# Attention and a two-part mixer: the channel mixer's pace in batches 2 and 3, and the row order of four heads' loads

## The chip, the cores and the metric

The kernel runs on one core of one Trainium2 chip. The metric is the device time of one launch in microseconds. Before the change it is 367.9 us, the median of 13 runs (366.7 to 375.08). The core's engines are TensorE (PE in the profile, with its weight loads as PEld), VectorE (DVE), ScalarE (ACT), GpSimd (POOL) and SyncE (SP); each takes its instructions in order and waits for the others by semaphores.

## The reference

Eight batches of eight heads, 576 tokens, head width 64. Causal attention with a decay bias is followed by a mixer over the sequence (low rank, 32) and a mixer over the channels:

```python
scores = scale * np.matmul(q, k.transpose(0, 1, 3, 2))
cum = np.cumsum(np.maximum(s, 0.0), axis=-1)
bias = -(cum[:, :, :, None] - cum[:, :, None, :])
scores = np.where(causal, -1e9, scores + np.minimum(bias, 0.0))
attn = softmax(scores)                    # with the row maximum and 1e-9
x = (attn @ v) heads side by side         # (8, 576, 512)
h = x.transpose(0, 2, 1) @ U @ V
u = x + h.transpose(0, 2, 1)
out = u + np.maximum(u @ w_ch1, 0.0) @ w_ch2      # 512 -> 2048 -> 512
```

Inputs and output are float32; the kernel works in bf16 and collects in float32.

## The kernel before, in words

**Attention** goes by pairs of heads, `n` = 0 to 31, four pairs a batch. `transposes(n)` turns q and k of a pair on TensorE (L314, 16 matmuls of 72 columns) into two PSUM banks; four copies on VectorE or ScalarE bring them to the pair's slot (L334 or L337). Which of the two lines runs depends on how q and k were loaded: in 72-token runs (L111: a partition holds tokens p, p + 72, and so on, in pieces of 64 numbers) the copy is straight (L334); with eight neighbouring tokens to a partition (L116: one piece of 512 numbers) the copy must put the tokens in order by a stride (L337). `in_runs` (L105) chooses, and is true for batches 3 to 7. For n = 4, 8, 9 and each batch's pair n % 4 == 2 above 8, ScalarE makes the copies of the first head. `scores(n)` is four steps of score matmuls (L401), each with an exponential on ScalarE (L416, L427, L433) and, for three of them, a causal mask on VectorE (L346). `values(n)` is two steps (one a head) of 15 matmuls (L461), each emptied by a reciprocal and a product on VectorE (L470, L471).

**The sequence mixer** `seqmix(b)` works on one batch: a product with U (L490), a small turn (L503), then the wide product with V (L535) into one score tile and two PSUM banks, and its last 64 tokens (L560). VectorE casts between them (uxT, L499; ux, L505) and adds x at the end (L515), which makes uT.

**The channel mixer** `chanmix(g)` works on groups of 512 tokens, nine in all, of which group b is complete when `seqmix(b)` is. It has 30 steps for groups 1 to 7. Sixteen are the *first product*: four matmuls of 512 columns (L647), then a ReLU on ScalarE (L807). Fourteen are the *second product*, done as seven products of half-size blocks (L692), eight matmuls of 256 columns to a step, with sums of blocks ahead of them (L674) and adds of results and of u behind them (L706), all on VectorE. Group 1's first eight steps also carry eight sums of weights on VectorE (L256). Each group's results go out from SP's queue (L716).

**Order.** PE's, VectorE's and the other engines' queues are in order. Attention's order is written out: up to pair 9 as words in `weave`, from `n = 8` on by the loop at L1008, which for each n takes transposes of n + 1, scores of n and values of n - 1. The channel mixer fills in between: after each attention step `step_fill` (L852) adds `pace[1]` to a counter and runs one channel mixer step whenever it reaches 16. So a pace of 11 gives 11 channel mixer steps to 16 attention steps. A batch's sequence mixer stands beside the next batch's second pair (`hp == 1`): its first two steps between attention steps, its other four with one channel mixer step after each (`fill_with(1)`). After it the next group is put on the list. What is left of the channel mixer when attention is done runs alone at the end.

**Buffers.** PSUM has four banks of one kind (`pwork`), shared by transposes, the scores' last piece, values, both channel products and the sequence mixer, and two score tiles of two banks each (`pscore`). q and k have two buffers each, filled a batch ahead from GpSimd's queue (L111, L116) with v behind them (L185); the loads for batch 2 are in two halves of four heads (`load(2)`, L965).

Of the kernel before, what the change touches and what calls it, by code (L numbers as in the profile page):

```python
# [39 lines left out]
def kernel(  # L40
# [40 lines left out]
    def pwork():  # L81
        return ps_w.tile([128, 512], FP32, tag="w", name="pwork")
# [19 lines left out]
        q_t[b] = loads.tile([TP, H, TT * D], BF16, tag="q_sd", name="q_sd")  # L102
        k_t[b] = loads.tile([TP, H, TT * D], BF16, tag="k_sd", name="k_sd")

    def in_runs(b):  # L105
        return b > 2

    def load_qk(b, h, n):
        for dst, src in ((q_t[b], q), (k_t[b], k)):
            if in_runs(b):  # L110
                nc.gpsimd.dma_start(  # L111
                    out=dst[:, ds(h, n), :].rearrange("p h (t d) -> p (h t) d", t=TT),
                    in_=src[b, ds(h, n)].rearrange("h (t p) d -> p (h t) d", p=TP),
                )
            else:
                nc.gpsimd.dma_start(  # L116
                    out=dst[:, ds(h, n), :],
                    in_=src[b, ds(h, n)].rearrange("h (p t) d -> p h (t d)", p=TP),
                )
# [6 lines left out]

    alloc_qk(0)
    load_qk(0, 0, 2)
    identity = consts.tile([128, 128], BF16)
    make_identity(nc, identity)  # L130
    load_qk(0, 2, 2)
    load_qk(0, 4, 2)
    load_qk(0, 6, 2)

# [44 lines left out]
    def load_v(b, parts=range(5)):  # L179
        vt = v_slot(b)  # L180
        if b < 3:
            init_v(nc.gpsimd, vt)
        for t in parts:
            rows_t = 128 if t < 4 else 64
            nc.gpsimd.dma_start(  # L185
                out=vt[:rows_t, t, :, 0:D],
                in_=v[b, :, ds(t * 128, rows_t), :].rearrange("h p d -> p h d"),
            )
# [14 lines left out]
    def slot_of(n):  # L203
        return slots[n % NSLOT if n < 2 * PB else (n + 1) % 3]
# [8 lines left out]
    def spin(n, dst):  # L213
        for _ in range(n):
            nc.tensor.matmul(  # L215
                dst, lhsT=busy[:, 0:128], rhs=busy[:, 0 : dst.shape[1]], start=True, stop=True
            )
# [70 lines left out]
    def copies(n, hh, par):  # L288
        b = n // PB
        on_act = hh == (n == 4) and ((n in (0, 1, 4, 8, 9) or n > 8 and n % PB == 2) or n == 2 and par == 0)  # L290
        return nc.scalar.copy if on_act else nc.vector.tensor_copy

    def transposes(n):
        b, hp = divmod(n, PB)
        slot = slot_of(n)
        if b > 0:
            for r, n_r, c in ((0, 3, 1), (3, 1, 0)):
                nc.sync.dma_start(
                    out=slot[ds(D + r, n_r), :, ds(c * S, S)],
                    in_=rows_hbm[ds(r, n_r), ds(2 * n, 2)],  # L300
                )
        tps = {}

        def turn(hh, c):
            if c == 0:
                tile = pwork()
                if (n, hh) == (3, 0):
                    spin(2, tile)
                tps[hh] = tile.bitcast(BF16)[:, : 2 * 4 * TP].rearrange(
                    "p (c t m) -> p c t m", c=2, t=4  # L310
                )
            src = (q_t[b], k_t[b])[c]
            for t2 in range(4):
                nc.tensor.transpose(  # L314
                    tps[hh][:, c, t2, :],
                    src[:, 2 * hp + hh, ds(t2 * 128, 128)],
                    identity[:TP, :TP],
                )

        if b == 0:  # L320
            for hh in range(2):
                turn(hh, 0)
            yield
        for hh in range(2):
            if b > 0:
                turn(hh, 0)
            turn(hh, 1)
            tp = tps[hh]
            dst = slot[0:D, hh, 0 : 2 * S]
            for par in range(2):  # L330
                src = tp[par * D : par * D + D]
                if in_runs(b):
                    by_run = dst.rearrange("p (c t two m) -> p c t two m", c=2, t=4, two=2)
                    copies(n, hh, par)(by_run[:, :, :, par, :], src)  # L334
                else:
                    in_turn = dst.rearrange("p (c m t two) -> p c m t two", c=2, t=4, two=2)
                    copies(n, hh, par)(  # L337
                        in_turn[:, :, :, :, par], src.rearrange("p c t m -> p c m t")
                    )
            yield  # L340
# [56 lines left out]
    def scores(n, pT, spins=()):  # L397
        slot = slot_of(n)

        def mm(dst, hh, j, lo, hi):  # L400
            nc.tensor.matmul(  # L401
                dst,
                lhsT=slot[0:KA, hh, ds(S + j * 128, 128)],
                rhs=slot[0:KA, hh, lo:hi],
                start=True,
                stop=True,
            )

        tail = None
        for hh in range(2) if n > 0 else ():  # L410
            near = pscore()
            for j in range(4):
                mm(near[:, ds(j * 128, 128)], hh, j, j * 128, j * 128 + 128)
            mm(near[:, 512:960], hh, 0, 128, S)
            mm(near[:, 960:1024], hh, 3, 512, S)
            nc.scalar.activation(pT[:, hh, 0:1024], near, EXP, scale=scale)  # L416
            if n >= PB:
                mask(pT[:, hh, 0:512].rearrange("p (a b) -> p a b", a=4), 4, 128)
            if spins:
                tail = tail or pwork()  # L420
                spin(spins[hh], tail)
            yield
        mid, tail = pscore(), tail or pwork()
        for hh in range(2):
            mm(mid[:, ds(hh * 512, 320)], hh, 1, 256, S)
            mm(mid[:, ds(hh * 512 + 320, 192)], hh, 2, 384, S)
        nc.scalar.activation(  # L427
            pT[:, :, 1024:1536], mid.rearrange("p (a b) -> p a b", a=2), EXP, scale=scale
        )
        yield  # L430
        for hh in range(2):
            mm(tail[:, ds(hh * 64, 64)], hh, 4, 512, S)
        nc.scalar.activation(  # L433
            pT[:, :, 1536:1600],
            tail[:, 0:128].rearrange("p (a b) -> p a b", a=2),
            EXP,
            scale=scale,
        )
        if n >= PB:
            mask(pT[:, :, 1536:1600], 2, 64)  # L440
        yield
# [408 lines left out]
    pace = [0, 16]  # L850

    def step_fill():  # L852
        pace[0] += pace[1]
        if pace[0] < 16:
            return
        pace[0] -= 16
        while fill:
            if next(fill[0], fill) is not fill:
                return
            fill.pop(0)  # L860

    def run(gen):
        for _ in gen:
            step_fill()
# [5 lines left out]
    def fill_with(n):  # L870
        per, pace[1] = pace[1], 16
        for _ in range(n):
            step_fill()
        pace[1] = per


    def pT_of(n):
        if n < PB + 3:
            return pTs[n % 2] if n % PB < 2 else pT_early[n % PB - 2]
        return pTs[(n + 1) % 2]  # L880

    def step(*gens):
        for gen in gens:
            next(gen, None)
# [80 lines left out]
    def load(b):  # L965
        alloc_qk(b)
        for h in range(0, H, 4 if b == 2 else H):
            load_qk(b, h, 4 if b == 2 else H)
# [35 lines left out]
    weave("V4 V4 S7 V5 S7 V5 S7 V6 S7 V6 T8 T8 V7 S8 V7 S8 T9 S8 T9")  # L1004
    weave("S8 S9 M1 S9 M1 S9 M1 M1 S9 M1 F M1")
    fill.append(chanmix(1))
    pace[1] = 11
    for n in range(2 * PB, NP + 2):  # L1008
        b, hp = divmod(n, PB)
        if hp == 0 and b < B - 1:  # L1010
            load(b + 1)
        mixing = seqmix(b - 1) if hp == 1 and b > FT else iter(())
        if b == B:
            fill_with(3)
            for _ in range(3):
                step(mixing)
                fill_with(2)
        if n > 2 * PB and n + 1 < NP:
            for at, _ in enumerate(transposes(n + 1)):
                step_fill()  # L1020
                if at == 0:
                    step(mixing)
        if 2 * PB + 1 < n < NP:
            for at, _ in enumerate(scores(n, pT_of(n))):
                step_fill()
                if at == 1:
                    step(mixing)
        for _ in mixing:
            fill_with(1)
        if hp == 1 and b > FT:  # L1030
            fill.append(chanmix(b - 1))
            pace[1] = 12
        if 2 * PB < n <= NP:
            run(values(n - 1, pT_of(n - 1)))
        if hp == 0 and 2 <= b < B - 1:
            load_v(b + 1)
# [35 lines left out]
```

The softmax here doesn't subtract the row's maximum and nothing guards it: scores larger than these inputs give would overflow.

## Time and profile before

| what | us |
|---|---|
| median of 13 runs | 367.9 |
| the profiled execution's own time | 368.34 |
| its span (first to last instruction) | 366.6 |
| PE busy | 356.3 |
| VectorE busy | 262.2 |
| ScalarE busy | 204.5 |
| GpSimd busy | 83.4 |
| L647, 560 matmuls of the first product | 136.3 |
| L692, L674, L706: the second product on PE, its sums and its adds on VectorE | see the groups by line |

A busy time is the sum of an engine's instructions, overlaps counted once. A group's row has the line, engine and operation, the tiles as out<-in with their shapes, the count, then busy us and mean ns of one, and behind the last bar the idle time ahead of these instructions with what ended it. A timeline's row has start and length in us; "x4" means four instructions of the kind in a row, and the bracket is the idle time before the first and what released it. Matmuls overlap in the pipeline and their ends are modelled, so PE's pace is read from starts.

### The profile page before, as it was taken

To read this page: it belongs to the slowest core of one execution; us is meant where nothing else is said; L and a number is where in the kernel's file an instruction comes from. 1 tells how busy PE (TensorE), PEld (TensorE's weight loads), DVE (VectorE), ACT (ScalarE), POOL (GpSimd) and SP (SyncE) were. 2 spreads that over 40 slices of the span, in tenths; PEclk is the share of its full clock that TensorE was granted. 3 is DMA by queue.
4 is the path that set the end of the run, shared out by engine and by line. 5 is a ranking of instruction groups with operands and counts; after the bars stand their busy time and mean duration, and the time that the engine had idled before them with its cause. 6 is when DMAs were issued, how large, how long until landed. Compare 5 with 4: busy or idle time off the path is not lost.

```text
span 366.6 us, 9426 instructions
## 1 busy us (share of the span) xinstructions
PE 356.3 (97%) x3959; PEld 248.6 (68%) x3959; DVE 262.2 (72%) x575; ACT 204.5 (56%) x309; POOL 83.4 (23%) x108
## 2 busy tenths in 40 slices
PE   8899999999999999999999999999999999999995
PEld 4675566665588667876679667876697568477484
DVE  8865776779798758995699559974897178076075
ACT  3874985756663578347843786357734630631720
POOL 8988435314030403140214022000000000000000
PEclk9999999999999999999999999999999999999999
DMA  7999999999949899989994999361014202403202
GB/s 109 168 205 201 165 192 104 147 129 142 98 44 91 145 142 63 99 90 115 140 100 65 142 132 84 58 156 22 18 48 118 64 18 84 91 5 109 61 29 88
DMA packets 147650, 37.40 MB, mean 102 GB/s; under 512 B 130648, under 2 KB 145976, under 8 KB 147608
## 3 DMA queue, kind: packets, MB, share of 16 engines
q0 software_dynamic: 104640, 18.49, 78.6%
q1 hardware_dynamic: 42680, 18.11, 27.3%
q8 instruction: 31, 0.51, 0.6%
q10 hardware_dynamic: 288, 0.20, 0.2%
q14 instruction: 11, 0.09, 0.1%
HBM read 37.25 MB, written 9.70 MB: 128 GB/s over the span
## 4 chain that ended last, share of the span: by engine, by line
PE 77%; DVE 12%; ACT 5%; issue 2%; DMA 2%; SPq 0%; DVEq 0%; ACTq 0%
PE pwork L647 29%; PE pwork L692 21%; PE pscore L401 9%; PE pwork L461 7%; PE pwork L314 3%; PE pwork L657 3%; DVE slot L337 2%; ACT hT L807 2%; DVE uT L515 2%; DVE o_sb L706 2%; ACT pT L416 2%; DVE slot L674 2%; DMA slot<-hT 2%; PE pscore L215 1%; PE pscore L647 1%
## 5 line engine op out<-in xcount | busy, mean ns | idle before, releaser
L647 PE MATMUL pwork<-uT,w_sb 128*128 128x512 bf16 x560 | 136.3, 379 | 1.5 <-DVE x_sb L471 0.8
L807 ACT ACTIVATE hT<-pwork 128x512 bf16<-128x512 f32 x140 | 84.3, 606 | 62.3 <-PE pwork L647 62.2
L416 ACT ACTIVATE pT<-pscore 128x1024 bf16<-128x1024 f32 x56 | 57.1, 1030 | 55.8 <-PE pscore L401 54.8
L647 PEld LDWEIGHTS <-w_sb 128*128 128x128 bf16 x576 | 50.7, 97 | 51.0 <-issue 1.2
L401 PE MATMUL pscore<-slot 68*128 68x320 bf16 (+1 forms) x500 | 56.1, 246 | 1.1 <-DMA slot<-hT 0.9
L401 PEld LDWEIGHTS <-slot 68*128 68x128 bf16 x564 | 41.3, 97 | 17.8 <-issue 1.3
L692 PEld LDWEIGHTS <-hT 128*128 128x128 bf16 x496 | 46.1, 98 | 7.5 <-issue 0.7
L185 POOL DMA_DIRECT2D v_slot<-in_v_dram x36 | 30.3, 857 | 85.2 <-PE pwork L461 74.6
L692 PE MATMUL pwork<-w_sb,hT 128*128 128x256 bf16 x384 | 47.5, 273 | 0.0
L346 DVE TENSOR_TENSOR pT<-pT,keep 128x512 bf16<-128x512 bf16 (+1 forms) x81 | 28.6, 353 | 20.7 <-ACT pT L416 14.9
L461 PEld LDWEIGHTS <-pT 128*128 128x128 bf16 x870 | 32.4, 97 | 5.3 <-issue 0.6
L461 PE MATMUL pwork<-v_slot,pT 128*128 128x65 bf16 x870 | 35.5, 194 | 0.2 <-DVE uT L515 0.2
L334 DVE COPY slot<-pwork 64x576 bf16<-64x576 bf16 x70 | 31.6, 452 | 4.5 <-PE pwork L314 3.9
L692 PE MATMUL pwork<-w_sum,slot 128*128 128x256 bf16 x256 | 31.5, 273 | 0.8 <-DVE o_sb L706 0.7
L471 DVE TENSOR_TENSOR x_sb<-pwork,rec 128x320 bf16<-128x320 f32 x64 | 31.1, 489 | 1.3
L337 DVE COPY slot<-pwork 64x576 bf16<-64x576 bf16 x35 | 28.0, 801 | 5.5 <-PE pwork L314 3.5
L427 ACT ACTIVATE pT<-pscore 128x1024 bf16<-128x1024 f32 x29 | 30.2, 1042 | 2.6 <-PE pscore L401 2.4
L674 DVE TENSOR_TENSOR slot<-hT 128x1024 bf16<-128x1024 bf16 x16 | 11.0, 688 | 24.5 <-ACT hT L807 24.3
L470 DVE RECIPROCAL rec<-pwork 128x5 f32<-128x5 f32 x64 | 12.0, 190 | 22.2 <-PE pwork L461 21.9
L692 PEld LDWEIGHTS <-slot 128*128 128x128 bf16 x256 | 24.0, 98 | 4.6 <-issue 1.6
L706 DVE TENSOR_TENSOR o_sb<-o_sb,pwork 128x512 f32<-128x512 f32 (+2 forms) x34 | 21.9, 650 | 1.0 <-PE pwork L692 0.3
L111 POOL DMA_DIRECT2D q_sd<-in_q_dram x5 | 11.2, 2239 | 43.0 <-PE pwork L314 43.0
(128 smaller groups left out, 417.5 us busy)
## 6 DMA issues: line engine op xcount, KB each, us to landing
out_dram<-o_sb SPq DMA_DIRECT2D x35, 256.0 KB
w_sb<-in_moe_w_ch_dram POOLq DMA_DIRECT2D x4, 1024.0 KB, 12.4
v_slot<-in_v_dram POOLq DMA_DIRECT2D x28, 128.0 KB, 6.8
q_sd<-in_q_dram POOLq DMA_DIRECT2D x5, 576.0 KB, 14.2
k_sd<-in_k_dram POOLq DMA_DIRECT2D x5, 576.0 KB, 17.6
q_sd<-in_q_dram POOLq DMA_DIRECT2D x4, 288.0 KB, 11.9
k_sd<-in_k_dram POOLq DMA_DIRECT2D x4, 288.0 KB, 11.6
q_sd<-in_q_dram POOLq DMA_DIRECT2D x4, 144.0 KB, 4.5
```

The source lines that it names most:

```text
L185: nc.gpsimd.dma_start(out=vt[:rows_t, t, :, 0:D], in_=v[b, :, ds(t * 128, rows_t), :].rearrange("h p d -> p h d"),)
L334: copies(n, hh, par)(by_run[:, :, :, par, :], src)
L337: copies(n, hh, par)(in_turn[:, :, :, :, par], src.rearrange("p c t m -> p c m t"))
L401: nc.tensor.matmul(dst, lhsT=slot[0:KA, hh, ds(S + j * 128, 128)], rhs=slot[0:KA, hh, lo:hi], start=True, stop=True,)
L416: nc.scalar.activation(pT[:, hh, 0:1024], near, EXP, scale=scale)
L427: nc.scalar.activation(pT[:, :, 1024:1536], mid.rearrange("p (a b) -> p a b", a=2), EXP, scale=scale)
L461: nc.tensor.matmul(po[:, i, :], lhsT=pT[:, hh, ds(place(j, i), 128)], rhs=vt[:, j, h, :], start=(j == 0), stop=(j == i), skip_group_check= ...
L471: nc.vector.tensor_tensor(x_sb[:, hp, :, ds(hh * D, D)], po[:, :, 0:D], rec.to_broadcast([128, 5, D]), op=ALU.mult,)
L647: nc.tensor.matmul(f1, lhsT=w1_sb[:, kt, ds(nf * 128, 128)], rhs=u[:, kt, :], start=(kt == 0), stop=(kt == 3),)
L692: nc.tensor.matmul(acc[:, i, :], lhsT=a[:, kt, ds(i * 128, 128)], rhs=b[:, kt, :], start=(i == 0 and kt == 0), stop=(kt == HF - 1), skip_g ...
L706: nc.vector.tensor_tensor(dst, a, b, op=ALU.add)
L807: nc.scalar.activation(hT[:, nf, :], f1, RELU)
```

## The change

Three things are changed. The pace of group 1's channel mixer during batch 2 goes from 11 to 6. The pace from batch 3's sequence mixer slot on (group 2) goes from 12 to 10, and stays 12 from batch 4's on. Heads 4 to 7 of batch 2 (pairs 10 and 11) are loaded in 72-token runs, as batches 3 to 7 are, so that their copies are the straight ones; heads 0 to 3 stay as they were.

```diff
-    def in_runs(b):
-        return b > 2
+    def in_runs(b, h):
+        return b > 2 or b == 2 and h >= 4
...
         for dst, src in ((q_t[b], q), (k_t[b], k)):
-            if in_runs(b):
+            if in_runs(b, h):
                 nc.gpsimd.dma_start(
...
                 src = tp[par * D : par * D + D]
-                if in_runs(b):
+                if in_runs(b, 2 * hp):
                     by_run = dst.rearrange("p (c t two m) -> p c t two m", c=2, t=4, two=2)
...
     fill.append(chanmix(1))
-    pace[1] = 11
+    pace[1] = 6
     for n in range(2 * PB, NP + 2):
...
         if hp == 1 and b > FT:
             fill.append(chanmix(b - 1))
-            pace[1] = 12
+            pace[1] = 10 if b < 4 else 12
         if 2 * PB < n <= NP:
```

## Prediction

> **What bounds the kernel now.** I read the page's first part, then its groups by line, then a table of busy time by stage, and last the timeline of the stages that were not full.
>
> ```profile
> PE 356.3 (97%) x3959; PEld 248.6 (68%) x3959; DVE 262.2 (72%) x575; ACT 204.5 (56%) x309; POOL 83.4 (23%) x108
> L334 DVE COPY slot<-pwork 64x576 bf16<-64x576 bf16 x70 | 31.6, 452 | 4.5 <-PE pwork L314 3.9
> L337 DVE COPY slot<-pwork 64x576 bf16<-64x576 bf16 x35 | 28.0, 801 | 5.5 <-PE pwork L314 3.5
> ```
>
> TensorE (PE) is issued nearly without a break, and the change neither adds nor removes a matmul. So the time can only move by PE's waits. The same copy of transposed q and k costs VectorE (DVE) 801 ns by stride (L337) and 452 ns in runs (L334).
>
> The stage table (stretch, its length, then busy time of PE, PEld, DVE, ACT, POOL) shows where PE waits:
>
> ```profile
> 78.50:102.30 23.80, 22.76 (x263) 13.90 (x261) 20.73 (x44) 16.27 (x26) 4.45 (x2) 1.00 1.96 117
> 102.30:118.00 15.70, 15.42 (x211) 13.39 (x210) 13.81 (x33) 7.85 (x12) 4.23 (x5) 1.00 0.86 68
> 118.00:141.00 23.00, 23.00 (x258) 14.93 (x256) 16.64 (x41) 15.50 (x25) 4.47 (x2) 1.00 1.51 134
> 182.00:195.00 13.00, 12.70 (x171) 10.80 (x170) 11.82 (x28) 5.20 (x8) 2.82 (x4) 1.00 1.24 87
> 220.00:234.00 14.00, 13.59 (x174) 11.11 (x171) 13.02 (x31) 5.84 (x10) 2.27 (x3) 1.00 0.98 78
> 256.00:270.00 14.00, 13.51 (x168) 10.07 (x165) 12.18 (x28) 7.95 (x13) 0.00 (x0) 1.00 0.06 13
> ```
>
> The first row is batch 2 beside group 1's first product, with DVE at 87%. The others that are not full hold a sequence mixer each, with DVE at 87 to 93%; between them (118 to 141) PE is full. The ends of matmuls are modelled and hide some 0.16 us of each wait, so I measure a wait from start to start: four 128x512 matmuls take 0.86 us, eight 128x256 take 0.88, a 15-matmul half of the values 0.46, four transposes 0.13, scores of a pair 1.38.
>
> ```profile
> 90.39 0.30 PE L314 MATMUL pwork<-identity,q_sd 72*128 72x72 bf16 x4
> 90.52 0.29 PE L314 MATMUL pwork<-identity,k_sd 72*128 72x72 bf16 x4
> 91.41 1.04 PE L647 MATMUL pwork<-uT,w_sb 128*128 128x512 bf16 x4 [0.60 <-DVE x_sb L471]
> ```
>
> ```profile
> 186.93 0.68 DVE L706 TENSOR_TENSOR o_sb<-U,u_sd 128x512 f32<-128x512 f32 x1
> 187.53 0.69 DVE L674 TENSOR_TENSOR v_slot<-hT,slot 128x1024 bf16<-128x1024 bf16 x1
> 188.13 0.22 DVE L346 TENSOR_TENSOR pT<-pT,keep 128x128 bf16<-128x128 bf16 x1
> 188.26 1.28 DVE L515 TENSOR_TENSOR uT<-pscore,xT 128x512 bf16<-128x512 f32 x2
> 189.46 0.75 DVE L515 TENSOR_TENSOR uT<-pwork,xT 128x256 bf16<-128x256 f32 x2
> 190.12 0.68 DVE L706 TENSOR_TENSOR o_sb<-o_sb,pwork 128x512 f32<-128x512 f32 x1
> ```
>
> At 90.52 the transposes would be through at 90.65; the next matmul starts at 91.41, so 0.76 us lost, because DVE had only just emptied the PSUM bank. At 188 the sequence mixer's uT adds stand in one queue with the second product's adds; the matmul that needs that bank starts at 190.85, 0.47 late.
>
> Such waits in all: batch 2 0.28 (80.3), 0.33 (83.3), 0.76 (90.6), 0.33 (99.8) = **1.7 us**; around sequence mixers 0.25 (112.8), 0.35 (116.9), 0.47 (190.4), 0.58 (230.2), 0.66 (261.8), 0.25 (302.8) = 2.56, of which 0.1 is a change of tile rows that stays: **2.45 us**. This 4.15 us is all that there is to win after 78 us; before that nothing is changed on PE.
>
> **What the Trainium skill says.** "TensorE: Matmul & The Clock Gate", section Back-to-back issue gap, gives N/2.4 + 2.5 ns between matmuls, 216 ns for 512 columns; the trace has 0.86/4 = 0.215 and agrees. (The shorter 131 ns that the section gives for streams with weight loads is not seen here.) "VectorE: DVE Perf Modes", What auto-detection actually checks, lets an all-16-bit op run at two elements a cycle only with step 1; the 801 against 452 ns above agree. "DMA: Bandwidth & Descriptors", Why small descriptors are slow, puts some 27% on a 256-byte piece: the direction agrees, the size I take from the trace below. "Perfetto Trace Analysis" calls matmul busy time a bad metric for closeness to the limit; hence starts, not busy shares, above.
>
> **The change part by part.** *Pace 6 for 11 in batch 2.* In the order of the built program, at the wide step of batch 2's sequence mixer (L535), group 1 has had 16 + 7 steps before the change and 13 after it: ten fewer. They move to the end of the program, where the last groups run alone at 0.86 and 0.88 us a step without gaps (the chain shows 64 matmuls in 13.81 and 112 in 12.23 us there): cost **0**, as PE does the same work.
>
> In batch 2 a pair now carries 3 steps of the first product and not 5.5. PE per pair: values 0.92, transposes 0.51, scores 1.38, 3 x 0.86 = 5.4 us. DVE per pair, in start-to-start distances read off its timeline (a row's mean is longer, since its ops overlap by 0.07 to 0.1): masks 0.34 + 0.34 + 0.14, values' reciprocals and products 1.04, copies 4 x 0.46, weight sums (L256) 3 x 0.60 = 5.5 us. So DVE keeps step within 2%. Before it had 0.82 + 1.04 + 4 x 0.80 + 5.5 x 0.60 = 8.4 against 7.6 of PE, and the 3 us by which it was behind at 92 us is what PE paid for. New there: ScalarE (ACT) gets a string of exponentials. From the end of the first score block to the bank that the first product wants after the values, ACT has 0.91 (exp) + 0.50 (ReLU) + 0.91 + 0.91 + 0.24 + 0.50 = 3.97 us after a start 0.2 later, PE 3.83: 0.35 late, once per pair, three times: 1.0 us. Batch 2: 1.7 becomes 1.0, **-0.7 us**.
>
> *Runs for pairs 10 and 11.* Eight copies; six on DVE fall from 0.80 to 0.46 = -2.0 us of DVE, two on ACT. Without it DVE would need 6.9 us in pair 11 against 5.4, so it is what makes the line above hold; no gain of its own beyond that. Cost: two loads (q and k, heads 4 to 7, 288 KB each) become 4608 rows of 256 bytes. Gpsimd issues them in about half of L111's 2.24 us each for eight heads, against 0.72: 2 x 0.4 = 0.8 us on a queue that waits anyway. On the DMA engines: from 55.4 (last piece of v for batch 2) to 83.7 us (v of batch 3 landed) q, k and v of batch 3, some 13,800 such rows, landed, 2.0 us a thousand, so 9.4 us; the long rows gave up 576 KB, which at the weight loads' 1024 KB in 12.4 us is 7.0. Net **+2.4**, bounded by 0 below and 9.4 above. What covers it: behind them are v of batch 2 (lands at 64.7, wanted at 79.9), and q and k of batch 3 (k issued at 59.97, lands 17.6 later at 77.6; wanted, in the new order, 7.7 us of PE after 78.5, so 86.2). The smaller slack is 8.6 us; the loads themselves land by 58.9, wanted at 78.5. Cost 0, at the upper end 0.8 us.
>
> *Every later sequence mixer* stands in the first product: in the built order the seven uT adds on DVE are now consecutive in all mixers from batch 2 to 7, and in most of them the cast ux stands ahead of any sum; before, 2 to 4 adds or sums of 0.6 us stood in between. Behind L535 PE now has three to four first-product steps, 2.6 to 3.5 us, which want ACT; the adds take 2.9 us on DVE. So 2.45 us of waits go. What is late next: the product steps all stand beside attention pairs, at pace 10 and 12. Per group DVE has 17 adds and sums x 0.605 = 10.3 plus 2.33 to 2.8 pairs x 3.7 = 18.9 to 20.7 us, PE 18.8 to 20.1: level, as before (19.4 against 19.0). I walked both orders with these distances, each engine taking its list in turn, and added how late each bank comes: before 6.8 us outside batch 2, of which the trace shows 2.85 with its small waits (0.42); after 4.4 us, spread as 0.4 to 0.6 over eight places, at the same ratio 1.85. That is -1.0; the count of waits removed says -2.45 at most. I take **-1.3**.
>
> *Pace 10 in batch 3* only keeps this offset. Queue order on SP: out stores move with the products, nobody waits for them.
>
> Sum: -0.7 - 1.3 = -2.0 us. The profiled run took 368.34 (span 366.6 and 1.7 around it), 0.44 above the median of 367.9; so 366.3 on its scale, **365.9** as a median.
>
> **Rivals.**
> (a) The waits change place only: ACT's string in batch 2 and the product steps beside scores cost what the mixers gave back. For: DVE's level load per group above; against: the uT run without sums. At no more than -0.7: 367.2 to 367.9, taken as 367.5.
> (b) Slower: DVE becomes the bound of the product phases, which now have none of their steps in a mixer's shadow. If its ops cost their full rows (0.69 an add, 4.2 a pair), DVE has 11.7 + 2.5 x 4.2 = 22.2 us against 19.3 of PE per group; once more than some 2 us behind (the time in which PE refills the four banks), PE pays about 1 us in each of groups 1 to 4: +4.0 - 0.7 (batch 2) - 1.0 (mixers) = +2.3, 370.2. Against it: back-to-back distances in DVE's timeline are 0.60, and before had the same load.
> (c) Larger gain: nearly all 4.15 go, and ACT's string hides in buffers: -3.8, 364.1.
> (d) The loads in runs come late: decides above 8.6 us, at most 0.8; an addition to any case, not a case.
>
> **How the numbers follow.** Forecast 0.41, (c) 0.15, (a) 0.28, (b) 0.16. About 0.5% (1.84 us) is what a measurement of this kernel can tell from no change. Forecast and (c) are faster by over that, just so for the forecast; hence 0.56, 0.28, 0.16. The range takes in (a), most of (c) and the near part of (b): 363.8 to 369.2. The forecast's own range is 364.8 to 366.6.
>
> **What would show it.** Right: PE full in the stretches of the mixers; seven uT adds in a row with no L706 or L674 among them; no L337 copy on DVE after batch 2's first two pairs and DVE below 95% there; T12's transposes not waiting for a DMA. Wrong: L692 waiting for DVE beside scores and values (b), L647 waiting for ACT L807 after values at many pairs (a), or PE waiting for k_sd at about 86 us (d).

## The result and the profile after

The changed kernel takes 371.35 us as a median (11 runs, 368.98 to 377.81) against 367.34 for the kernel before (48 runs). The ratio is 1.0091, interval 1.0071 to 1.0111: slower by some 3.3 us, where 2.0 us less was forecast. Medians and ratios differ a little because executions in which the chip was disturbed count in the medians, not in the ratios.

The profiled execution took 370.23 us (span 368.5), 1.1 below its median, while the one of before lay 1.0 above its own. So the two traces show only 1.9 us of the loss, and I use them for places and mechanisms; sizes come from the timed runs.

The page's busy row and the two copy rows of the kernel after:

```profile
PE 357.4 (97%) x3959; PEld 247.9 (67%) x3959; DVE 261.5 (71%) x575; ACT 203.8 (55%) x309; POOL 84.7 (23%) x108
L334 DVE COPY slot<-pwork 64x576 bf16<-64x576 bf16 x76 | 34.3, 451 | 2.5 <-PE pwork L314 1.6
L337 DVE COPY slot<-pwork 64x576 bf16<-64x576 bf16 x29 | 23.3, 802 | 5.1 <-PE pwork L314 3.3
```

The instructions are the same in number. Six copies on VectorE moved from L337 to L334 and cost what they cost before. So nothing was added to the work; PE waits more.

The table by stage of the kernel after (stretch, length, busy of PE, PEld, DVE, ACT, POOL, then clock, DMA share, GB/s). The stretches are those of before by work: batch 2, its sequence mixer, the stretch behind it, then the sequence mixers of batches 4, 5 and 6:

```profile
78.00:98.00 20.00, 19.77 (x273) 13.35 (x272) 17.98 (x48) 16.13 (x25) 5.21 (x3) 1.00 2.15 128
98.00:112.00 14.00, 11.91 (x150) 8.03 (x148) 10.93 (x27) 7.63 (x13) 3.47 (x5) 1.00 1.63 79
112.00:135.00 23.00, 23.00 (x328) 18.87 (x325) 19.90 (x48) 13.07 (x19) 7.81 (x6) 1.00 1.57 148
170.00:184.00 14.00, 12.82 (x133) 6.95 (x132) 7.13 (x20) 9.20 (x16) 2.71 (x4) 1.00 1.25 111
206.00:220.00 14.00, 13.99 (x173) 9.15 (x170) 9.70 (x25) 8.15 (x13) 4.22 (x5) 1.00 1.22 151
244.00:258.00 14.00, 14.00 (x177) 10.00 (x174) 11.39 (x29) 7.32 (x11) 0.00 (x0) 1.00 0.50 107
```

The last two rows are what was forecast: mixers in which PE is busy throughout and VectorE at 69 and 81%. The second and the fourth are the surprise. PE is idle for 2.1 and 1.2 us there, while VectorE is at 78% and 51%. No engine is the bound in these stretches.

The list of waits of the kernel after, from 78 us on, names what is late (who <- for what: us in all, times, longest). The list of before has no row in which anything waits for xT:

```profile
DVE uT L515 <- DMA xT<-x_sb: 3.7, 2, 2.1
...
PEld L461 <- DVE uT L515: 3.1, 2, 1.6
...
PE pwork L461 <- DVE uT L515: 2.3, 2, 1.2
```

xT is x turned by a DMA: behind the values of each pair SP issues a DMA transpose (L478, in the last lines of `values`) into the pair's fourth of xT, and the uT adds of the sequence mixer add it. At two mixers the last pair's fourth was not there when its three adds came up. VectorE's timeline shows both places:

```profile
103.83 1.28 DVE L515 TENSOR_TENSOR uT<-pscore,xT 128x768 bf16<-128x768 f32 x2
105.03 0.74 DVE L515 TENSOR_TENSOR uT<-pwork,xT 128x384 bf16<-128x384 f32 x2
107.35 1.09 DVE L515 TENSOR_TENSOR uT<-pwork,xT 128x384 bf16<-128x384 f32 x3 [1.58 <-DMA xT<-x_sb]
...
176.54 1.28 DVE L515 TENSOR_TENSOR uT<-pscore,xT 128x512 bf16<-128x512 f32 x2
177.74 0.74 DVE L515 TENSOR_TENSOR uT<-pwork,xT 128x256 bf16<-128x256 f32 x2
180.61 1.09 DVE L515 TENSOR_TENSOR uT<-pwork,xT 128x256 bf16<-128x256 f32 x3 [2.13 <-DMA xT<-x_sb]
```

The seven adds do stand in a row, as the built order said. Their first four run; the last three wait. The bank that they should empty is wanted next by the values. PE's timeline of the kernel after, at both places:

```profile
105.96 1.04 PE L692 MATMUL pwork<-w_sb,hT 128*128 128x256 bf16 x8
108.16 1.09 PE L461 MATMUL pwork<-v_slot,pT 128*128 128x65 bf16 x30 [1.17 <-DVE uT L515]
...
110.10 0.29 PE L314 MATMUL pwork<-identity,k_sd 72*128 72x72 bf16 x4
110.77 1.05 PE L692 MATMUL pwork<-w_sb,hT 128*128 128x256 bf16 x8 [0.38 <-DVE x_sb L471]
...
179.27 1.03 PE L647 MATMUL pwork<-uT,w_sb 128*128 128x512 bf16 x4
181.42 1.09 PE L461 MATMUL pwork<-v_slot,pT 128*128 128x65 bf16 x30 [1.13 <-DVE uT L515]
```

From start to start, 105.96 to 108.16 is 2.20 against 0.88, so 1.3 us lost, and 179.27 to 181.42 is 2.15 against 0.86, again 1.3. At 110.10 the transposes take 0.67 instead of 0.13: VectorE, set back by its wait, is late with the next bank as well.

Why is x's transpose late? The chain that ended last, in the window of each mixer, gives the way from issue to landing (start, length, what):

```profile
98.19 8.69 DMA xT<-x_sb
...
171.54 8.98 DMA xT<-x_sb
```

Around the second of them, SP's queue of the kernel after reads:

```profile
168.44 3.00 SPq L814 DMA_TRANSPOSE u_sd<-uT  x1
171.54 1.58 SPq L478 DMA_TRANSPOSE xT<-x_sb  x1
```

and in the kernel before, at the same mixer, nothing stands ahead of the last x:

```profile
181.99 1.24 SPq L478 DMA_TRANSPOSE xT<-x_sb  x1
```

VectorE's last three adds start there without a wait:

```profile
190.72 1.08 DVE L515 TENSOR_TENSOR uT<-pwork,xT 128x256 bf16<-128x256 f32 x3
```

In the kernel before, x's last values were ready at 181.96 and the transpose went out at 181.99. In the kernel after they were ready at 169.44 and it went out at 171.54, 2.1 us later, because SP was inside the transpose of u (L814). The channel mixer issues that in its fourth step (`nf == 3`), so it goes wherever the pace puts that step; here it fell just ahead of the last x.

The wait on SP is only half of it. The trace also records when a DMA has completed. In the kernel before, this x landed at 189.08, 7.1 us after its issue; in the kernel after at 180.52, 9.0 us after it. The DMA packets show what lay between: u's 2048 pieces of 256 bytes run from 169.7 to 174.3 us, and x's 640 only from 175.6 to 178.2. From x ready to x landed that makes 7.1 us before and 11.1 us after.

At batch 2's mixer nothing stood ahead on SP (98.17 ready, 98.19 issued). There the DMA engines were full. GpSimd's queue of the kernel after shows when the loads were issued:

```profile
83.59 2.22 POOL L111 DMA_DIRECT2D k_sd<-in_k_dram  x1
97.25 4.22 POOL L185 DMA_DIRECT2D v_slot<-in_v_dram  x5 [11.43 <-PE pwork L461]
```

The view of the DMAs gives 19.7 us from issue to landing for this k load (batch 4's), so until 103.3; v, which waits for the same last values as x, goes out beside it and takes 9.3 us at the median. v goes out beside x (108.19) in the kernel before too:

```profile
106.40 4.23 POOL L185 DMA_DIRECT2D v_slot<-in_v_dram  x5 [18.18 <-PE pwork L461]
```

What differs is the k load. In the kernel before the same view, from 94 to 107 us in 40 slices, has the DMA engines' busy tenths as

```profile
DMA  9999999999999999999510399400000000000002
```

so they were idle from 102.5 us until v went out, and x's turn came at 108.19; it landed 5.3 us later. From the issue of that k load to x's last transpose there were 22.2 us before (86.00 to 108.19) and are 14.6 now. The Trainium skill, "Perfetto Trace Analysis", Per-instruction lifecycle, warns that for a DMA the whole data movement lies outside the instruction's row. This case agrees: SP's row at 98.19 is 1.22 us, the data came 8.69 us after it began. Nor is it a matter of the transpose's rate: "DMA: Bandwidth & Descriptors", Latency and other measured facts, has 261 GB/s for a DMA transpose, by which the 160 KB of one pair (128 partitions x 640 bf16) would move in an estimated 0.6 us. No run here shows that rate, but in batches 6 and 7 of the kernel after, where no load runs beside it, x landed 2.6 us after its issue.

### The profile page after: what moved, and what is told of

It is laid out like the page before. It is cut to its first block, busy times and chain, and to the rows that moved or that the text cites. A ratio compares the mean times of both kernels' runs of the same rounds, so it can differ in the third digit from the quotient of the medians.

```text
span 368.5 us, 9439 instructions
## 1 busy us (share of the span) xinstructions
PE 357.4 (97%) x3959; PEld 247.9 (67%) x3959; DVE 261.5 (71%) x575; ACT 203.8 (55%) x309; POOL 84.7 (23%) x108
## 4 chain that ended last, share of the span: by engine, by line
PE 78%; DMA 7%; ACT 6%; DVE 5%; issue 2%; SPq 0%; POOL 0%; DVEq 0%; ACTq 0%; POOLq 0%
PE pwork L647 27%; PE pwork L692 25%; PE pscore L401 9%; PE pwork L461 6%; DMA xT<-x_sb 5%; PE pwork L314 3%; PE pwork L657 3%; ACT pT L416 2%; ACT hT L807 1%; DMA slot<-hT 1%; DVE slot L674 1%; DMA k_sd<-in_k_dram 1%; PE pscore L647 1%; ACT pT L427 1%; DVE slot L337 1%
## 5 line engine op out<-in xcount | busy, mean ns | idle before, releaser
L647 PE MATMUL pwork<-uT,w_sb 128*128 128x512 bf16 x560 | 133.6, 379 | 1.1 <-ACT pT L433 0.5
L416 ACT ACTIVATE pT<-pscore 128x1024 bf16<-128x1024 f32 x56 | 55.8, 1028 | 36.7 <-PE pscore L401 36.3
L401 PE MATMUL pscore<-slot 68*128 68x320 bf16 (+1 forms) x500 | 53.5, 246 | 0.4 <-DMA slot<-hT 0.2
L346 DVE TENSOR_TENSOR pT<-pT,keep 128x512 bf16<-128x512 bf16 (+1 forms) x81 | 28.2, 352 | 21.3 <-ACT pT L416 11.1
L334 DVE COPY slot<-pwork 64x576 bf16<-64x576 bf16 x76 | 34.3, 451 | 2.5 <-PE pwork L314 1.6
L461 PEld LDWEIGHTS <-pT 128*128 128x128 bf16 x870 | 30.6, 97 | 7.3 <-DVE uT L515 3.1
L461 PE MATMUL pwork<-v_slot,pT 128*128 128x65 bf16 x870 | 32.5, 194 | 2.3 <-DVE uT L515 2.3
L427 ACT ACTIVATE pT<-pscore 128x1024 bf16<-128x1024 f32 x29 | 30.1, 1039 | 0.8 <-PE pscore L401 0.6
L337 DVE COPY slot<-pwork 64x576 bf16<-64x576 bf16 x29 | 23.3, 802 | 5.1 <-PE pwork L314 3.3
L111 POOL DMA_DIRECT2D q_sd<-in_q_dram x6 | 12.6, 2105 | 45.8 <-PE pwork L314 40.7
L314 PEld LDWEIGHTS <-q_sd 72*128 72x128 bf16 x256 | 14.9, 97 | 7.4 <-DMA q_sd<-in_q_dram 1.0
## 6 DMA issues: line engine op xcount, KB each, us to landing
q_sd<-in_q_dram POOLq DMA_DIRECT2D x5, 576.0 KB, 11.1
```

Source lines behind the costliest of these rows:

```text
L337: copies(n, hh, par)(in_turn[:, :, :, :, par], src.rearrange("p c t m -> p c m t"))
L346: nc.vector.tensor_tensor(dst, dst, keep[:, :, 0:w].to_broadcast([128, n_tiles, w]), op=ALU.min)
L401: nc.tensor.matmul(dst, lhsT=slot[0:KA, hh, ds(S + j * 128, 128)], rhs=slot[0:KA, hh, lo:hi], start=True, stop=True,)
L427: nc.scalar.activation(pT[:, :, 1024:1536], mid.rearrange("p (a b) -> p a b", a=2), EXP, scale=scale)
L461: nc.tensor.matmul(po[:, i, :], lhsT=pT[:, hh, ds(place(j, i), 128)], rhs=vt[:, j, h, :], start=(j == 0), stop=(j == i), skip_group_check= ...
L647: nc.tensor.matmul(f1, lhsT=w1_sb[:, kt, ds(nf * 128, 128)], rhs=u[:, kt, :], start=(kt == 0), stop=(kt == 3),)
```

## The experiments

My theory after the traces was that the loss is the last x coming late, at batch 4 by u's transpose on SP, at batch 2 by the loads. The rivals: VectorE or ScalarE as the bound of the new order (rivals (a) and (b) of the prediction), and the loads in runs. Every kernel is timed in five rounds beside the kernel before on the same chip; ratios are against that. One per cent is 3.7 us.

### The two parts alone

`pace_only` keeps the new paces and loads batch 2 as before; `runs_only` keeps the loads in runs and the old paces.

```diff
# pace_only, against the kernel after
-        return b > 2 or b == 2 and h >= 4
+        return b > 2
# runs_only, against the kernel after
-    pace[1] = 6
+    pace[1] = 11
...
-            pace[1] = 10 if b < 4 else 12
+            pace[1] = 12
```

Expected of `pace_only`:

> The paces 6 and 10 without the loads in runs. Theory: the loss of 3.3 us is the late DMA transpose of the last pair's x (xT), which two of the mixers' last adds wait for (1.6 and 2.1 us idle on VectorE in the profile), and it comes with the pace: this one loses as much or more, 1.009 to 1.014, the more by VectorE's strided copies in batch 2 (2 us of copies come back). Rival, the loads in runs delay something on the DMA queues: then this is at 1.000 to 1.003.

Expected of `runs_only`:

> The loads in runs with the old paces 11 and 12. Theory: 0.996 to 1.000, since VectorE is 3 us behind in batch 2 and gets 2 us less to do, of which PE sees up to 0.8. Rival (the loads cost DMA time that somebody waits for): 1.004 to 1.009.

Measured: `pace_only` 371.29 us, ratio 1.0093 (1.0068 to 1.0117); `runs_only` 366.59, ratio 0.9970 (0.9947 to 0.9993). The whole loss comes with the pace. In the trace of `pace_only` PE waits for x at batch 4 alone (1.39 us); in batch 2 it waits for VectorE instead (0.96 us at 87.5), which has the strided copies back. The loads in runs by themselves gain 0.3%, 1.1 us, and add nothing measurable when the pace is there too (1.0091 beside 1.0093). Where the 1.1 us come from is seen in PE's timeline of `runs_only`, at the place where the prediction found 0.76 us lost before (90.52 to 91.41):

```profile
89.44 0.29 PE L314 MATMUL pwork<-identity,k_sd 72*128 72x72 bf16 x4
89.78 1.04 PE L647 MATMUL pwork<-uT,w_sb 128*128 128x512 bf16 x4
```

0.34 instead of 0.89 from start to start. All waits of PE after 78 us, measured start to start, sum to some 6.0 us before, 4.8 in `runs_only` and 9.1 after.

### Without the last x

The adds of the last pair take the fourth of the pair before it, and the last 64 tokens' add takes other columns of xT. This leaves the last pair's x out of u; all instructions stay.

```diff
-                nc.vector.tensor_tensor(dst, src, xT[:, dt, lo:hi], op=ALU.add)
+                x_in = xT[:, 2 if dt == 3 else dt, lo:hi]
+                if lo == 512:
+                    x_in = xT[:, 0, 0:256].rearrange("p (a b) -> p a b", a=4)
+                nc.vector.tensor_tensor(dst, src, x_in, op=ALU.add)
```

> The changed kernel in which the mixer's last two kinds of adds take x of an earlier pair in place of x of pairs 6 and 7 of heads (the fourth quarter of the channels gets the third quarter's x, the last 64 tokens get other tokens' x): same adds, same sizes, but nothing waits for the last DMA transpose of a batch. Theory: the waits of 1.33 us (106.7) and 1.29 us (179.9) on PE go, with those like them in other executions, ratio 0.999 to 1.003. Rival (ScalarE's strings in batch 2, or product steps beside attention, are the loss): 1.007 to 1.010.

Measured: 367.59 us, ratio 0.9986 (0.9966 to 1.0006). Against the kernel after that is 1.05% less, some 3.8 us: the wait for the last x is the loss. In its trace PE's two waits of 1.3 us are gone and that of 0.54 is down to 0.2; the sum of PE's waits is some 6.1 us.

The same edit on `runs_only`, as a control:

> The runs with the old paces, and nothing waiting for the last transpose of x (the fourth quarter takes the third's x, the last tokens other tokens' x). In that order the last x has 7 to 9 us to land and no wait for it shows. Theory: the same as the runs alone, 0.996 to 0.998, so that the new paces are worth nothing by themselves (0.9986 with them). If waits for x are hidden in the old order too: 0.990 to 0.994.

Measured: 366.12 us, ratio 0.9967 (0.9960 to 0.9974), as `runs_only`. In the trace of `runs_only` nobody waits for x. The control also says something else: without the last x, the new paces stand at 0.9986 and the old ones at 0.9967. Even freed of the new wait, the new paces gain nothing over the old.

### What makes the last x late: two edits, to u's transpose and to v's load

`after_v_late` writes v's load one pair later into the program for the batches concerned. `after_u_behind_x` moves u's transpose from the channel mixer's 4th step to its 11th, and keeps SP's DMA transposes in the order in which they are written (`in_program_order` ties each to the one before). `after_u_and_v` does both.

```diff
# after_v_late
-        if hp == 0 and 2 <= b < B - 1:
+        if hp == 1 and 2 < b < B - 1 or n == 2 * PB:
# after_u_behind_x
-            if g > 0 and nf == 3:
+            if g > 0 and nf == 10:
...
+    in_program_order(tc, traced, [E.SP], "Transpose")
```

Expected of `after_v_late`:

> The changed kernel with the loads of v for batches 4 to 7 issued one pair later, so that they do not run on the DMA engines at the same time as the last transpose of x. Theory, if the transpose is slow because it shares the engines with v (queue 0 had about 1000 packets a us in 104 to 107 us): the transpose lands in 5 to 6 us, not 8.7, and the ratio is 1.000 to 1.004. If it takes that long by itself, or by its place in SP's queue: 1.007 to 1.010.

Of `after_u_behind_x`:

> The changed kernel with the DMA transpose of u (L814) asked for at the first product's 11th step, not its 4th, and held to the written order among the DMA transposes on SP's queue, so that it never stands ahead of a batch's last transpose of x. In the profile of the changed kernel it did in batch 4: x ready at 169.44, its transpose issued at 171.54, behind one of u that took 3.0 us. Theory: that wait on PE (1.29 us) goes, batch 2's stays: ratio 1.003 to 1.006. If SP's queue is no part of it: 1.008 to 1.011.

Of `after_u_and_v`:

> As the last one, and v of batches 4 to 7 loaded one pair later too. With v late alone the wait at batch 2 had gone from the profile (landed by 7.3 us, not 8.7) and that at batch 4 had stayed. Theory: both causes of a late transpose are gone, ratio 0.998 to 1.002, as in the kernel that leaves the last x out (0.9986). If the transpose is simply longer than the way from the values to the adds: 1.005 or more.

Measured: v late 370.82 us, ratio 1.0079 (1.0054 to 1.0105), not to be told from the kernel after. u behind x 367.95, 1.0032 (1.0012 to 1.0051), 0.6% or 2.2 us less. Both 367.77, 1.0009 (0.9999 to 1.0018), 0.8% or 3.0 us less.

The edit of v moved nothing. GpSimd's queue in the trace of v late:

```profile
98.40 4.23 POOL L185 DMA_DIRECT2D v_slot<-in_v_dram  x5 [11.43 <-PE pwork L461]
```

x went out at 99.35 there, so v went out 0.95 us ahead of it, as in the kernel after (97.25 and 98.19); at batch 4 v goes out 0.95 us before x is ready in both. GpSimd has nothing else to do between the two places and waits in either for the values that free v's buffer, so v goes out at the same time. By their traces, v late is thus the kernel after a second time, and "both" is u behind x a second time. What v costs beside x no run here shows; the 0.1 and 0.2% between the twins show what a repeat can differ by.

At batch 4 the cause is u. With u behind x, SP's queue sends x the moment it is ready (170.66):

```profile
170.69 1.24 SPq L478 DMA_TRANSPOSE xT<-x_sb  x1
```

and VectorE's adds there wait for PE only:

```profile
177.76 1.28 DVE L515 TENSOR_TENSOR uT<-pscore,xT 128x512 bf16<-128x512 f32 x2
178.96 1.41 DVE L515 TENSOR_TENSOR uT<-pwork,xT 128x256 bf16<-128x256 f32 x4
180.69 0.42 DVE L515 TENSOR_TENSOR uT<-pwork,xT 128x256 bf16<-128x256 f32 x1 [0.32 <-PE pwork L560]
```

From x ready to x landed it takes 10.2 to 11.2 us in the five traces with 6 in batch 2 in which u stands ahead, 4.7 to 5.6 in the three in which u is held back, and 6.5 to 7.4 in the kernel before and the four others with the old paces. Holding u back gives 2.2 us in one run and 3.0 in its twin, of the 3.8 that leaving x out gives: it is the larger part.

At batch 2 the cause stays open. There v late still has u and v where they were, and yet its x landed 6.6 us after its issue and nothing waited: the wait comes and goes between executions of one order. What the traces of all fourteen kernels show is that a longer time goes together with the k load of batch 4. In five of them that load had landed before the last x went out, and x landed 5.3 to 5.7 us after its issue; in the other nine, the eight with 6 in batch 2 and `all_runs`, it was still under way, and x took 6.2 to 8.7 us. v goes out beside x in all fourteen. The adds reach for this x some 7.6 us after its issue, and PE lost time behind them in three traces, those with the longest times: the kernel after, `six_then_twelve` (0.43 us) and `all_runs` (below). No run moves the k load alone.

The edit of u on the old paces, `runs_u_behind_x`:

> Old paces, heads 4 to 7 of batch 2 in runs, and u's transpose held behind x's on SP's queue. Theory: in the old order no transpose of x waits behind one of u long enough for PE to see it, so 0.995 to 0.998 as the runs alone. If the old order also paid for it in executions that the profile doesn't show: 0.992 to 0.995.

Measured: 366.57 us, ratio 0.9979 (0.9961 to 0.9996), not to be told from `runs_only`. The order on SP is worth something only where u stands in front of a last x.

### The two paces apart

`six_then_twelve` keeps 6 in batch 2 and the old 12 after it; `eleven_then_ten` keeps 11 in batch 2 and the 10 in batch 3.

```diff
# six_then_twelve
-            pace[1] = 10 if b < 4 else 12
+            pace[1] = 12
# eleven_then_ten
-    pace[1] = 6
+    pace[1] = 11
```

Expected of `six_then_twelve`:

> Pace 6 in batch 2, 12 from batch 3 on; runs as changed. The way from the last values to the mixer's adds is set by how many channel mixer steps stand between, so batch 2 is as in the changed kernel and batch 4's mixer meets other steps. Theory: 1.003 to 1.010, the upper part if batch 4's transpose again stands behind one of u. Rival (the loss is made in batch 3's pace 10): 0.997 to 1.000.

Of `eleven_then_ten`:

> Pace 11 in batch 2 as before, 10 in batch 3; runs as changed. Batch 2's mixer is then the old one, whose last x has 7.7 us to land. Theory: 0.996 to 1.001, like the runs alone (0.997), with at most one late transpose in a later batch. Rival (pace 10's product steps beside attention are the loss): 1.004 to 1.009.

Measured: 370.51 us, ratio 1.0092 (1.0072 to 1.0113), and 367.57, ratio 1.0010 (1.0002 to 1.0018). The 6 in batch 2 is what costs. With 12 behind it the offset of the groups changes, and x's last transpose at batch 4 is still issued 2.2 us after x is ready (173.16 to 175.33), behind u's, which takes 5.77 us there, and what was queued after it. In its trace PE loses little at the adds themselves (0.43 us at batch 2, nothing at batch 4, but 0.67 at 186.3 for VectorE, set back by its wait), so this run shows which pace costs, not how. The 10 alone gives back what the runs gain: its trace has 0.66 to 0.73 us of waits at four mixers (152.3, 184.0, 221.3, 258.6).

### ScalarE's string in batch 2

On top of `after_u_and_v`, the third exponential of pairs 10 to 13 works on 256 of its 1024 columns. This leaves three quarters of that exponential out in four pairs.

```diff
+        w = 128 if 10 <= n <= 13 else 512
-            pT[:, :, 1024:1536], mid.rearrange("p (a b) -> p a b", a=2), EXP, scale=scale
+            pT[:, :, 1024 : 1024 + w],
+            mid.rearrange("p (a b) -> p a b", a=2)[:, :, 0:w],
+            EXP,
+            scale=scale,
```

> The changed kernel with u behind x and v late (1.0009), and in pairs 10 to 13 the third exponential works on 256 of its 1024 columns (the rest of those weights are left as earlier pairs left them), so that ScalarE has some 0.6 us less a pair beside batch 2. Theory: what is left of the loss is ScalarE's string, which holds the first product's bank three times by 0.5 us and once, at the wide step, by 0.72: most of these 2.2 us go, ratio 0.995 to 0.998. Rival (VectorE holds them, or they are made up elsewhere): 0.9995 to 1.002.

Measured: 366.86 us, ratio 0.9995 (0.9975 to 1.0014), 0.14% under `after_u_and_v` with intervals that overlap: inconclusive as a time. The waits that it was to remove, in PE's timeline of the kernel after:

```profile
85.24 0.29 PE L314 MATMUL pwork<-identity,k_sd 72*128 72x72 bf16 x4
85.60 1.02 PE L647 MATMUL pwork<-uT,w_sb 128*128 128x512 bf16 x4
...
86.72 0.61 PE L401 MATMUL pscore<-slot 68*128 68x128 bf16 x6
87.31 1.02 PE L647 MATMUL pwork<-uT,w_sb 128*128 128x512 bf16 x4
...
102.32 0.39 PE L535 MATMUL pwork<-V_sb,ux 32*128 32x512 bf16 x2
103.25 2.75 PE L647 MATMUL pwork<-uT,w_sb 128*128 128x512 bf16 x12 [0.55 <-ACT pT L433]
```

Four transposes take 0.36 instead of 0.13, six score matmuls 0.59 instead of 0.44: with 0.1 more at the values, about 0.5 us a pair in batch 2, and 0.72 at the mixer (0.93 less 0.22), where the bank is free only after ScalarE's last exponential. In `short_exp` the first two together are down to 0.1 a pair and the last to 0.1. But further on in PE's timeline of `short_exp` a bank emptied by VectorE is late:

```profile
108.43 0.29 PE L314 MATMUL pwork<-identity,k_sd 72*128 72x72 bf16 x4
109.49 1.05 PE L696 MATMUL pwork<-w_sb,hT 128*128 128x256 bf16 x8 [0.77 <-DVE x_sb L475]
```

1.06 instead of 0.13 (lines are four further down in that kernel), a wait of 0.9 where 0.2 stood in `after_u_and_v`. My reading, not tested, is that PE gets there earlier and VectorE does not; what is shown is only that the one wait shrank and the other grew.

### A version that beats both

`all_runs` keeps the old paces and loads all of batch 2 in runs.

```diff
# against runs_only
-        return b > 2 or b == 2 and h >= 4
+        return b >= 2
```

> Old paces, all heads of batch 2 loaded in runs. VectorE has 2.1 us less to copy (six of the eight copies of pairs 8 and 9; the other two are ScalarE's), beside group 0's second product, where PE waits little. Expected 0.995 to 0.998; if the loads come late for pair 8 (they land at 54.8, wanted at 62): 1.000 or more.

Measured: 365.88 us, ratio 0.9967 (0.9951 to 0.9984). It beats the kernel before by 0.33% and the kernel after by 1.2%; from `runs_only` it can't be told. Four more copies on VectorE are short (L334 has 80), not six: ScalarE makes four of the eight. Its trace has a new wait of PE of 1.27 us at 114.6, and that is the last x again, with the old paces:

```profile
114.57 0.56 DVE L515 TENSOR_TENSOR uT<-pwork,xT 128x384 bf16<-128x384 f32 x1 [0.83 <-DMA xT<-x_sb]
```

It was issued at 105.92 and landed 8.6 us later. So a late x at batch 2 is not bound to the new paces, and this version has some of the same loss in it.

## Why the prediction was wrong

**The step that failed** is the one sentence "Queue order on SP: out stores move with the products, nobody waits for them". It counts the stores and puts the rest of that queue at nothing. SP's queue carries x's transposes (L478) and u's (L814) too, and the mixer's adds want the first of these some 8 to 9 us after x is ready. At batch 4 the adds of before took it up at 190.72, 8.8 us after x was ready; it had landed after 7.1 us, with 1.6 to spare. Those of after wanted it at 178.48, 9.0 us after x was ready, and it landed after 11.1, because u's transpose had come in between: 2.1 us of waiting on SP and 1.9 us more from issue to landing. At batch 2 the time from issue to landing rose from 5.3 to 8.7 us, of some 7.6 that are free; the k load for batch 4, issued 14.6 us ahead of x and not 22.2, was still landing, but that it is the cause is not shown. Neither the queue nor this way had a price in the sum, nor did the rivals hold it: the slower one was put on VectorE, which was at 51 to 78% where the time was lost.

The result lies 5.3 us from the forecast (3.3 more where 2.0 less was forecast). Leaving out the last x gives back 3.8 of them. The other 1.5 belong to the sizes of the two terms of the sum:

**Batch 2.** The mechanism was right (VectorE keeps up, ScalarE's string is late once a pair), the size was not: 0.35 a pair was forecast, about 0.5 measured, and the wait of 0.72 for ScalarE at the wide step (L535) was not in the list. Waits of 1.7 us became 2.2, not 1.0.

**The mixers.** The waits of before at 112.8 to 302.8, 2.45 us in sum, are gone, the uT adds stand in a row, and batches 5 and 6 show PE busy throughout. In their place are the two waits for xT (1.33 and 1.29), three behind transposes, for a bank of the values (0.54 and 0.47 at 110.2 and 152.5 in the second product, 0.48 at 228.8 in the first), and some 0.4 us in the wide step itself at three mixers (138.1, 175.8 and 214.4), whose last matmul waits for a bank that ScalarE's ReLU empties. The second of these three, and the same step in the kernel before:

```profile
175.81 0.81 PE L535 MATMUL pwork<-V_sb,ux 32*128 32x512 bf16 x2
176.55 0.82 PE L647 MATMUL pwork<-uT,w_sb 128*128 128x512 bf16 x3
...
187.19 0.39 PE L535 MATMUL pwork<-V_sb,ux 32*128 32x512 bf16 x2
187.51 0.72 PE L692 MATMUL pwork<-w_sb,hT 128*128 128x256 bf16 x5
```

From the step's start to the next product it is 0.74 against 0.32. In all that makes 5.3 us of new waits, where some 1.2 was expected to stay. Rival (a), that the waits change place only, holds for what is left once x is in time: `after_u_and_v` is at 1.0009 and `after_no_last_x` at 0.9986.

**The runs.** "No gain of its own" was wrong for the runs alone, which gain 1.1 us at the old pace, and right beside pace 6. That their DMA cost is covered was right: no wait for q or k in the trace of after.

**Pace 10** was to keep the offset at no cost. Alone it costs 0.4% against `runs_only`; behind the 6 it makes no difference (1.0091 and 1.0092).

What stays open: leaving out the last x gives 3.8 us, while the profiled execution shows 2.6 us of PE waiting for it, and 0.3 to 0.4 more behind it. The twin `after_v_late` shows only 1.45. That other executions lose more is inferred; no trace of such a one was taken. A third place may take part: at batch 3's mixer u also stands ahead (x ready at 132.37, sent at 133.57), and x landed at 139.86, 0.8 us before its add; in the twin VectorE waits 0.77 us for it there, PE not. How much of batch 2's lateness is the k load, how much v and how much u is not separated either.

## What to carry to other kernels

When steps are moved in a filled schedule, list every queue in which they issue something, DMA transposes and loads included, and for each the time from its input to its use: here 7 us of the 9 that were free, until a neighbour on the queue added 4. A stretch that becomes shorter also brings its successor's inputs closer to loads that start as before. When an experiment moves an issue, read in its trace whether it went out at another time: v did not, since its queue waits in both places for the same values. And a wait that moves between engines is gone only when the next queue in line has slack; try the parts alone, for here the smaller one carried the only gain.

## What was not expected of the hardware

- One pair's x, 160 KB turned by a DMA transpose between places in SBUF, lands 2.6 us after its issue where no load runs beside it (batches 6 and 7 of the kernel after). Beside loads of short rows it took 5.3 to 7.1 us in the kernel before (batches 2 to 5) and 8.7 and 9.0 at the two late places of the kernel after. SP's row is 1.2 to 1.6 us in each of these.
- A transpose of u holds SP for 2.0 to 6.3 us in one and the same kernel (3.00 at 168.44), and one of x behind it waits until that has ended, even when its data is ready; its own pieces then move only after u's (175.6 after 174.3 us).
- A 576 KB load in pieces of 64 numbers (L111) took 19.7 us from issue to landing when another of its kind was issued 2.2 us ahead of it.
